# A new order of steps for a fused attention and Fourier-mixing kernel

## The chip, the cores and the metric

The kernel runs on one core of one Trainium2 chip. The metric is the device time of one execution in microseconds. The engines are TensorE (PE, with its weight loads as PEld), VectorE (DVE), ScalarE (ACT), GpSimd (POOL) and SyncE (SP, which here only issues DMAs).

## What is computed

For 4 batches, 8 heads, 768 positions and head size 64, block-sparse attention: each query sees its own block of 64 keys and the three blocks with the highest gate score, causally. Its result, 768 x 512 per batch, goes through a two-dimensional Fourier transform (the real part), a layer norm and a two-layer network with a residual:

```python
gate_scores = np.einsum('bhsd,bhnd->bhsn', q, k_rep)       # k_rep: mean of k over blocks of 64
top_idx = np.argsort(gate_scores, axis=-1)[..., -top_k:]   # causal, top_k = 3, own block always
attn = softmax(scale * q @ k.T under that mask); x = attn @ v
mixed = np.real(np.fft.fft(np.fft.fft(x, axis=1), axis=2)); u = x + mixed
un = (u - mu) / np.sqrt(var + 1e-06)
out = u + np.maximum(un @ w_ch1, 0.0) @ w_ch2              # 512 -> 2048 -> 512
```

## The kernel before

The work is cut into 16 head pairs P (batch P // 4) for the attention and 4 batches b for the rest. Each piece is a named step, and the string `ORDER` lists all steps, `name:arguments`, in one sequence. A loop at the end of the kernel calls each step's function; every engine then executes its own instructions in the order in which the list issues them, whatever the scheduler would choose, and SP its DMAs likewise. So the list is five queues written as one. Engines wait for each other only through the data and through buffers: PSUM has four slots of two banks that tp, g, sc, av, yp, mx, xt, h and c tiles share; the q/k slots `qk_s` are three (P % 3), the v slots four, the loaded q and k have three buffers each, the loaded v two.

The steps, by engine:

- SP: `Lq`, `Lk`, `Lv` load a pair; `un` for batches 1 to 3 is two DMA transposes; `od` stores 128 rows.
- PE: `tk`, `tq` transpose k and q of pair P (L297; up to P = 8 and 6); `g` gate scores (L347, L354); `s:P,i` one of six score tiles (L421 with mask matmuls L433 for P < 7, L426 after that); `v` attention times v (L461); `y:b,h` and `m:b,kp` the two transforms (L531/L537, L564/L565); `xt` transposes of batch 0 (L597); `w:b,it` one of 16 slices of the first layer (L641/L643); `c:b,st,h` half of one row tile of the second layer (L668).
- DVE: `ks`, `kh` block sums of k; `qc` q copied or turned (L328, L326); `kb` turns k; `gt`, `gx`, `gl`, `gm` threshold and mask of the gate (L361/L366, L378, L221, L398); `x` divides the attention (L472, L221); `fs`, `fd`, `f` fold x for the transform (L221 and short copies L506 to L516); `tr` a reversed copy; `u` adds x (L578); `bn`, `nv` statistics (L610 to L621); `un` for batch 0 (L602); `r:b,it` with it % 4 = 3 (L651); `o` scales and adds (L680).
- ACT: `kc` copies k (L317, L320); `e:P,i` the exponential of a score tile (L443); `ty` a copy; `xu` (L590); the other `r` (L653).
- POOL: `qs` q into its slot; `d:P,i` the causal triangle of a tile (L449); `vc` the cast of v; `K` the mask rows for P >= 7 (eight copies through L224); `nr` a Newton iteration (12 small steps); `W`, `X` issue the loads of the weights; `pg:b` copies four elements of the folded tile, so POOL stands there until the fold of batch b is finished (L519).

An attention pair goes through Lk/Lq, tk/tq, ks/kh/qc, g, gt, gx, gl, gm, (K), s, e, d, v, x. A batch goes through fs, fd (pairwise adds and differences), f, y, ty/tr, m, u, xu, un, then w/r, c, o, od, with bn, nv, nr beside w. The pairs of the next batch are interleaved with w and c of the one before.

Of the kernel before, what the change touches and what calls it, by code (L numbers as in the profile page):

```python
# [117 lines left out]
gl:2,1 e:1,2 d:1,3 gm:2 g:3 d:1,4 ks:4 d:1,0 v:0 d:1,5 gt:3 vc:1 kc:4 gx:3 e:1,1 s:2,5 Lv:3 Lq:6
LF:0 Lq:7 Lk:6 Lk:7 LT:0 s:2,3 kh:4 gl:3,0 e:2,5 gl:3,1 s:2,4 e:2,3 d:1,1 x:0 tq:5 qs:4 e:2,4 g:4
d:2,3 gm:3 qc:5 s:2,0 d:2,4 s:2,2 d:1,2 e:2,0 gt:4 d:2,5 tk:5 vc:2 gx:4 e:2,2 s:2,1 ks:5 d:2,0 Lv:4  # L120
Lq:8 Lk:8 s:3,1 e:2,1 v:1 gl:4,0 kh:5 gl:4,1 kc:5 d:2,1 gm:4 d:2,2 s:3,2 x:1 e:3,1 vc:3 g:5 e:3,2
Lv:5 Lc:0 d:3,1 s:3,5 gt:5 s:3,0 fs:0,1 e:3,5 s:3,3 d:3,2 gx:5 e:3,0 s:3,4 fs:1,1 tq:6 gl:5,0 e:3,3
fs:0,0 v:2 gl:5,1 fs:1,0 e:3,4 d:3,3 qc:6 d:3,0 s:4,5 x:2 d:3,4 s:4,4 e:4,5 d:3,5 s:4,0 qs:5 v:3
# [22 lines left out]
un:1,1 un:1,2 un:1,0 od:0,3 Lk:13 Lk:14 od:0,5 Lv:12 od:0,4 Lv:13 Lk:15 Lq:15 od:0,2 w:1,0 x:9 g:12
s:11,2 s:11,4 e:10,5 s:10,4 w:1,12 e:10,3 gt:12 e:10,0 w:1,10 s:11,1 e:10,2 e:11,0 s:11,5 w:1,1
r:1,0 e:11,2 s:10,1 kb:13 ks:13 gx:12 gl:12,0 fs:9,1 gl:12,1 gm:12 kb:14 qc:13 kh:13 fs:9,0 fs:8,0
w:1,8 e:10,4 e:11,4 w:1,11 r:1,12 r:1,11 r:1,10 e:11,5 r:1,1 s:11,3 e:10,1 w:1,6 qc:14 ks:14 kh:14
w:1,15 w:1,13 r:1,8 kc:13 g:14 e:11,3 g:13 e:11,1 r:1,15 gt:13 r:1,6 gx:13 bn:1,4 gl:13,0 gl:13,1  # L150
w:1,5 gm:13 d:11,5 d:10,5 d:10,1 d:10,4 d:10,2 d:11,4 K:12 d:11,3 d:10,3 d:11,2 d:11,0 d:10,0 K:13
# [648 lines left out]
```

## Time and profile before

| | |
|---|---|
| device time, median of 3 runs | 292.67 us (292.5 to 293.05) |
| profiled execution: device time | 292.97 us |
| its span | 291.2 us |
| PE, DVE, ACT, POOL busy | 276.6, 202.9, 163.6, 116.1 us |
| mean granted TensorE clock | 1.0 |

A row of the profile names line, engine, operation, the tile written and the tiles read. "Idle" is the time an engine stood before an instruction, and the releaser is the instruction whose end let it go on. Steps share helper lines (L221 for all two-operand steps, L224 for copies on POOL), so they are told apart by tile. The clock was the same in every stretch.

### The profile page before, as it was taken

To read this page: it belongs to the slowest core of one execution; us is meant where nothing else is said; L and a number is where in the kernel's file an instruction comes from. 1 tells how busy PE (TensorE), PEld (TensorE's weight loads), DVE (VectorE), ACT (ScalarE), POOL (GpSimd) and SP (SyncE) were. 2 spreads that over 40 slices of the span, in tenths; PEclk is the share of its full clock that TensorE was granted. 3 is DMA by queue.
4 is the path that set the end of the run, shared out by engine and by line. 5 is a ranking of instruction groups with operands and counts; after the bars stand their busy time and mean duration, and the time that the engine had idled before them with its cause. 6 is when DMAs were issued, how large, how long until landed. Compare 5 with 4: busy or idle time off the path is not lost.

```text
span 291.2 us, 6585 instructions
## 1 busy us (share of the span) xinstructions
PE 276.6 (95%) x2537; PEld 169.2 (58%) x2537; DVE 202.9 (70%) x604; ACT 163.6 (56%) x205; POOL 116.1 (40%) x286
## 2 busy tenths in 40 slices
PE   8799999899998989999998999999999999999994
PEld 4466777655665465556574466656676454564642
DVE  2999999999996978977899766793566155420231
ACT  3698989865872625978577672864263401353100
POOL 2267527454888650852771798038000000003000
PEclk9999999999999999999999999999999999999999
DMA  9999999998999297259610002543000331000063
GB/s 199 278 225 228 205 200 205 221 170 155 172 174 194 65 222 131 51 123 242 109 41 2 0 7 50 146 91 146 0 2 0 37 109 36 0 2 0 0 237 127
DMA packets 118287, 33.52 MB, mean 115 GB/s; under 512 B 111024, under 2 KB 115056, under 8 KB 118256
## 3 DMA queue, kind: packets, MB, share of 16 engines
q1 hardware_dynamic: 112592, 28.47, 45.0%
q0 software_dynamic: 3664, 4.19, 8.8%
q10 hardware_dynamic: 2000, 0.44, 0.7%
q8 instruction: 20, 0.33, 0.5%
q14 instruction: 11, 0.09, 0.1%
HBM read 28.63 MB, written 6.29 MB: 120 GB/s over the span
## 4 chain that ended last, share of the span: by engine, by line
PE 68%; DVE 17%; ACT 8%; POOL 4%; issue 2%; DVEq 0%; ACTq 0%; POOLq 0%
PE c L668 24%; PE h L641 15%; PE h L643 7%; ACT pt L443 5%; PE sc L426 5%; PE av L461 4%; DVE kr L306 2%; PE yp L531 2%; PE mx L564 2%; POOL pt L449 2%; DVE q L328 2%; PE mx L565 2%; DVE mx L378 1%; PE warmps L705 1%; DVE u L578 1%
## 5 line engine op out<-in xcount | busy, mean ns | idle before, releaser
L443 ACT ACTIVATE pt<-sc 128x1024 f16<-128x1024 f32 (+1 forms) x96 | 82.8, 921 | 28.9 <-PE sc L426 19.8
L641 PE MATMUL h<-unT,w 128*128 128x512 f16 x256 | 84.8, 379 | 2.3 <-DVE hT L651 1.1
L668 PE MATMUL c<-w_sb,hT 128*128 128x512 f16 x368 | 84.0, 379 | 0.5 <-ACT hT L653 0.5
L643 PE MATMUL h<-unT,w 128*128 128x256 f16 x256 | 69.7, 272 | 0.0
L653 ACT ACTIVATE hT<-h 128x768 f16<-128x768 f32 x48 | 37.6, 809 | 51.4 <-PE h L643 51.2
L449 POOL TENSOR_SCALAR_AFFINE_SELECT pt<-pt 128x256 f16<-128x256 f16 x96 | 40.0, 444 | 49.1 <-ACT pt L443 48.6
L668 PEld LDWEIGHTS <-hT 128*128 128x128 f16 x368 | 35.4, 98 | 40.0 <-issue 1.2
L641 PEld LDWEIGHTS <-w 128*128 128x128 f16 x256 | 25.0, 97 | 29.5 <-issue 1.2
L651 DVE TENSOR_SCALAR hT<-h 128x768 f16<-128x768 f32 x16 | 15.1, 948 | 27.3 <-PE h L643 27.3
L680 DVE SCALAR_TENSOR_TENSOR u<-c,rs,u 128x512 f32<-128x512 f32 (+1 forms) x25 | 17.5, 721 | 20.3 <-PE c L668 19.2
L643 PEld LDWEIGHTS <-w 128*128 128x128 f16 x256 | 25.0, 98 | 6.0 <-issue 2.6
L224 POOL TENSOR_SCALAR_AFFINE_SELECT qk<-q 64x768 f16<-64x768 f32 (+1 forms) x25 | 21.5, 862 | 15.0 <-DVE q L328 11.0
L426 PE MATMUL sc<-qk 96*128 96x512 f16 (+3 forms) x144 | 26.2, 306 | 0.0
L224 POOL TENSOR_SCALAR_AFFINE_SELECT qk<-mt 32x160 f16<-32x160 f16 x72 | 23.1, 341 | 7.6 <-DVE mt L398 5.8
L221 POOL TENSOR_TENSOR t<-vr,rs 128x6 f32<-128x6 f32 x12 | 2.9, 242 | 54.5 <-DVE rs L621 53.8
L461 PEld LDWEIGHTS <-pt 128*128 128x128 f16 x672 | 22.4, 97 | 3.0 <-issue 0.8
L461 PE MATMUL av<-v,pt 128*128 128x65 f16 x672 | 23.2, 193 | 0.6 <-POOL v L224 0.6
L578 DVE SCALAR_TENSOR_TENSOR u<-mx,x 128x512 f32<-128x512 f32 x24 | 15.6, 687 | 8.4 <-PE mx L565 8.4
L590 ACT ACTIVATE x<-u,nm 128x512 f16<-128x512 f32 x24 | 15.7, 714 | 9.7 <-DVE nm L584 9.5
L426 PEld LDWEIGHTS <-qk 96*128 96x128 f16 x144 | 13.1, 97 | 9.9 <-issue 1.2
L421 PE MATMUL sc<-qk 64*128 64x512 f16 (+3 forms) x112 | 14.7, 306 | 1.8 <-ACT pt L443 0.8
L610 DVE BATCH_NORM_STATS2 bst<-u 128x6 f32<-128x512 f32 x24 | 16.2, 674 | 0.0
(99 smaller groups left out, 357.2 us busy)
## 6 DMA issues: line engine op xcount, KB each, us to landing
nat<-in_v_dram SPq DMA_DIRECT2D x16, 384.0 KB, 4.3
out_dram<-u SPq DMA_DIRECT2D x23, 256.0 KB, 2.7
nat<-in_q_dram SPq DMA_DIRECT2D x36, 96.0 KB, 4.0
nat<-in_k_dram SPq DMA_DIRECT2D x17, 192.0 KB, 3.4
nat<-in_k_dram SPq DMA_DIRECT2D x28, 96.0 KB, 2.8
nat<-in_q_dram SPq DMA_DIRECT2D x13, 192.0 KB, 3.6
...
```

What stands on the lines that cost most here:

```text
L224: nc.gpsimd.affine_select(out=out, in_=in_, pattern=[[0, i] for i in n], base=0, channel_multiplier=0, compare_op=ALU.is_ge, fill=0.0)
L426: nc.tensor.matmul(ps[:, e, co:co + q1 - q0], qk[0:96, e, 1, 128 * jt:128 * jt + 128], qk[0:96, e, 0, q0:q1], start=True, stop=True)
L443: nc.scalar.activation(out=d["pt"][:, o:o + 2 * n].rearrange("p (e c) -> p e c", e=2), in_=d["sc", i][:, :, 0:n], func=AF.Exp, scale=0.125)
L449: nc.gpsimd.affine_select(out=dg, in_=dg, pattern=[[0, 2], [1, 128]], base=0, channel_multiplier=-1, compare_op=ALU.is_ge, fill=0.0)
L461: nc.tensor.matmul(av[:, e, 66 * st:66 * st + 65], pt[:, co:co + 128], vv[:, e, jt, 0:65], start=(cnt == 0), stop=(cnt == 20))
L578: nc.vector.scalar_tensor_tensor(out=u_b[:, k2, :].rearrange("p (m two) -> p two m", two=2), in0=mps[:, k2, :].rearrange("p (two m) -> p t ...
L610: nc.vector.bn_stats(out=bst, in_=u_t[b, kt // 2][:, kt % 2, :])
L641: nc.tensor.matmul(hp[:, 0:512], w1s, unT[:, dt, 0:512], start=(dt == 0), stop=(dt == NDT - 1))
L643: nc.tensor.matmul(hp[:, 512:768], w1s, unT[:, dt, 512:768], start=(dt == 0), stop=(dt == NDT - 1))
L653: nc.scalar.activation(out=hT, in_=hp, func=AF.Relu)
L668: nc.tensor.matmul(c_ps[b, g[0]][:, st - g[0], :], h_t[b, it][:, 128 * st:128 * (st + 1)], w2_sb[:, it, :], start=(it == 0), stop=(it == N ...
L680: nc.vector.scalar_tensor_tensor(out=o, in0=ps, scalar=st_t[b][1][:, st:st + 1], in1=o, op0=ALU.mult, op1=ALU.add)
```

## The change

The set of steps and everything each step does stay the same, as do the constants and first loads ahead of the list. Only `ORDER` differs, from its first line to its last: every engine's queue, and SP's, has another order, made with the knowledge that VectorE and GpSimd can lock each other out. The core of the diff (old lines first, then new ones; each "..." stands for lines left out):

```diff
@@ ORDER = """
-Lk:1 Lq:1 Lk:2 Lq:2 tk:0 ks:0 tq:0 Lq:3 Lk:3 kh:0 qc:0 iz:1 tk:1 qs:0 kc:0 g:0 ks:1 iz:0 gt:0 tq:1
-kc:1 gx:0 Lq:4 Lv:0 Lk:4 Lv:1 kh:1 gl:0,0 tk:2 gl:0,1 gm:0 kc:2 qc:1 s:0,3 s:0,2 ks:2 e:0,3 qs:1
...
-fs:3,0 s:5,2 fd:2,1 e:5,0 fd:3,1 s:4,3 fd:3,0 e:5,2 tk:6 f:0,1 f:0,2 e:4,3 Lk:9 Lq:9 tk:7 f:0,3
-e:4,2 f:0,0 y:0,1 ks:7 pg:0 W:0 kc:6 y:0,0 tr:0,1 d:4,0 kc:7 d:4,4 d:4,5 ks:6 d:5,5 d:4,1 ty:0,1
-tr:0,0 s:5,3 d:5,2 s:5,4 d:4,3 kh:6 W:1 ty:0,0 m:0,2 qs:6 e:5,3 u:0,2 m:0,1 vc:4 e:5,4 m:0,0 u:0,1
-xu:0,2 d:5,4 tk:8 d:5,1 d:4,2 u:0,0 xu:0,1 d:5,0 xt:0,2 W:2 g:6 un:0,2 xu:0,0 xt:0,1 gt:6 un:0,1
-kc:8 xt:0,0 qc:8 un:0,0 qs:8 v:4 Lq:10 Lk:10 Lv:6 Lq:11 qc:7 bn:0,3 gx:6 w:0,1 gl:6,0 r:0,1 w:0,2
-gl:6,1 gm:6 r:0,2 w:0,5 s:6,0 s:6,3 w:0,6 ks:8 kh:7 x:4 kh:8 bn:0,4 g:8 g:7 fs:4,1 s:6,1 r:0,5 e:6,0
...
-bn:0,0 bn:0,2 ks:10 gl:9,0 fs:5,1 nv:0 gl:9,1 e:7,1 s:7,2 e:7,2 gm:9 qs:9 K:8 d:7,3 d:6,3 d:6,2
-d:6,5 d:6,0 d:7,4 vc:6 d:7,2 d:6,1 d:7,5 X:1 qs:10 K:9 vc:7 d:7,0 d:7,1 nr:0 kc:9 s:8,3 w:0,9 r:0,9
-w:0,14 r:0,14 w:0,11 v:6 s:8,5 r:0,11 kh:10 w:0,15 g:10 e:8,3 e:8,5 c:0,0,0 x:6 s:9,1 v:7 s:8,4
-fs:6,1 gt:10 c:0,1,0 s:8,2 c:0,2,0 s:8,1 s:8,0 r:0,15 fs:6,0 x:7 c:0,0,1 s:9,5 c:0,1,1 fs:7,0 gx:10
-fs:7,1 fd:7,1 fs:4,0 fd:6,0 qc:11 fd:7,0 fd:6,1 f:1,1 f:1,0 f:1,2 f:1,3 y:1,1 e:9,1 e:8,4 e:8,2
...
-vc:8 vc:9 d:8,3 d:8,1 d:8,4 d:9,5 qs:11 d:8,5 d:9,1 d:9,3 d:9,4 d:8,0 d:9,0 vc:10 K:10 qs:12 d:9,2
-pg:1 K:11 vc:11 v:8 s:10,5 c:0,4,1 s:10,3 s:10,0 x:8 o:0,4 o:0,5 kb:12 ks:12 kh:12 v:9 s:10,2 s:11,0
...
-c:1,0,1 s:12,3 e:12,5 e:13,4 s:13,0 e:12,3 s:13,1 kc:15 e:13,1 c:1,1,1 c:1,4,0 e:13,0 gx:15 fs:8,1
-fs:11,1 fd:11,1 gl:15,0 fd:10,0 fd:11,0 fd:10,1 f:2,1 f:2,2 gl:15,1 gm:15 f:2,0 f:2,3 nr:1 d:12,0
-d:12,1 d:13,3 d:13,2 d:13,5 d:12,3 qs:15 d:12,5 d:12,4 d:12,2 vc:12 d:13,0 K:15 K:14 pg:2 d:13,1
-d:13,4 vc:13 y:2,0 v:12 c:1,4,1 ty:2,0 y:2,1 o:1,0 s:15,3 tr:2,0 c:1,5,0 ty:2,1 m:2,0 c:1,5,1 o:1,1
...
+Lk:1 Lq:1 Lk:2 Lq:2 Lq:3 Lk:3 tk:0 kc:0 ks:0 tq:0 iz:0 kh:0 qc:0 tk:1 ks:1 g:0 iz:1 kc:1 tq:1 tk:2
+gt:0 gx:0 gl:0,0 gl:0,1 kh:1 gm:0 kc:2 qc:1 qs:0 qs:1 Lq:4 Lv:0 Lk:4 Lv:1 Lq:5 Lk:5 s:0,3 tq:2 s:0,4
...
+e:5,3 f:0,3 f:0,2 gx:6 f:0,0 gl:6,0 f:0,1 y:0,1 qc:8 gl:6,1 tr:0,1 y:0,0 e:5,2 tr:0,0 e:4,1 e:5,1
+tk:8 ks:8 gm:6 e:4,4 m:0,2 kh:7 W:0 W:1 d:4,2 pg:0 d:4,1 d:4,3 vc:4 d:4,0 d:4,4 d:4,5 d:5,3 W:2 v:4
+u:0,2 ty:0,1 ty:0,0 m:0,0 s:6,2 x:4 u:0,0 kc:8 g:7 kh:8 m:0,1 gt:7 xu:0,2 xt:0,2 e:6,2 u:0,1 s:6,5
+s:6,0 xu:0,0 e:6,5 un:0,2 s:6,1 xt:0,0 gx:7 s:6,3 un:0,0 e:6,0 g:8 gl:7,0 xu:0,1 gt:8 xt:0,1 s:6,4
+s:5,0 un:0,1 w:0,9 e:6,3 e:5,0 bn:0,3 gl:7,1 gm:7 kb:9 bn:0,1 e:6,4 w:0,2 Lq:10 Lk:10 Lv:6 Lq:11
+d:6,0 vc:5 d:5,1 qs:8 d:5,4 d:5,2 K:7 d:5,0 d:5,5 X:0 d:6,5 qs:7 Li:0 Lv:7 Lq:12 Lv:8 Lv:9 r:0,2
...
+ks:10 kh:10 r:0,10 g:9 w:0,1 r:0,11 qc:11 r:0,14 w:0,13 gt:9 gx:9 gl:9,0 bn:0,2 nv:0 gl:9,1 gm:9
+d:7,5 d:7,2 d:6,2 d:6,3 d:7,0 d:6,4 qs:9 X:1 vc:6 d:7,3 K:8 d:6,1 d:7,1 vc:7 d:7,4 K:9 nr:0 r:0,13
+w:0,0 r:0,0 v:6 r:0,1 s:8,4 e:8,4 s:8,3 x:6 w:0,7 v:7 e:8,3 s:8,5 qc:10 fs:6,1 r:0,7 c:0,0,0 s:9,4
+s:8,1 e:8,1 c:0,1,0 c:0,1,1 s:9,0 e:9,4 e:9,0 c:0,0,1 s:9,1 x:7 fs:7,1 fs:6,0 fd:6,1 fs:5,1 fd:6,0
+fs:7,0 fd:7,1 fd:7,0 f:1,3 f:1,2 Lv:10 Lv:11 Lk:11 Lq:13 Lq:14 Lk:12 g:10 e:8,5 y:1,1 s:8,2 f:1,1
...
+ks:12 kh:12 u:1,0 kc:12 xu:1,0 gl:11,0 g:12 c:0,4,1 gt:12 u:1,2 gl:11,1 gm:11 xu:1,2 d:8,3 vc:8
+d:8,4 vc:9 pg:1 vc:10 qs:11 d:8,5 d:8,0 d:9,4 d:9,3 K:10 vc:11 qs:12 qs:10 d:8,1 d:9,2 d:8,2 d:9,5
+K:11 d:9,0 d:9,1 od:0,2 od:0,1 od:0,0 Lk:13 un:1,1 un:1,0 un:1,2 Lk:14 Lv:12 Lv:13 Lk:15 Lq:15
...
+fd:10,1 gm:14 s:13,4 c:1,1,0 s:12,1 c:1,1,1 e:13,4 gl:15,0 f:2,3 gl:15,1 f:2,0 f:2,2 gm:15 bn:1,2
+nv:1 f:2,1 e:13,3 c:1,0,1 y:2,1 e:13,1 e:12,1 y:2,0 tr:2,0 kc:15 ty:2,1 kc:14 c:1,4,0 ty:2,0 c:1,5,0
+s:13,2 e:13,2 d:12,0 d:12,2 d:12,4 K:14 d:12,3 d:13,5 d:12,1 nr:1 d:13,3 qs:15 d:12,5 K:15 d:13,4
+d:13,0 d:13,2 qs:14 pg:2 d:13,1 v:12 s:15,4 o:1,1 c:1,5,1 s:15,1 tr:2,1 m:2,1 e:15,4 o:1,0 x:12
...
```

More of the change, by code (lines that the diff above doesn't have):

```diff
@@ L118 @@
[L118 to L123, printed above, removed]
@@ L146 @@
[L146 to L151, printed above, removed]
@@ new lines @@
+kb:13 e:10,5 v:9 s:11,0 e:10,1 e:11,0 w:1,0 r:1,0 s:11,2 w:1,10 s:11,1 x:9 e:11,2 s:11,5 e:11,5
+w:1,2 s:10,0 w:1,15 s:10,4 e:11,1 w:1,13 fs:9,0 gl:12,1 s:11,4 o:0,5 s:11,3 kb:14 ks:13 r:1,15
+bn:1,4 ks:14 r:1,2 kh:13 fs:9,1 bn:1,1 qc:14 gm:12 w:1,1 w:1,12 e:10,0 e:10,4 g:13 gt:13 r:1,10
+w:1,11 e:11,4 gx:13 gl:13,0 r:1,11 gl:13,1 gm:13 e:11,3 bn:1,5 d:11,5 vc:13 d:10,1 qs:13 d:10,4
+vc:12 d:11,2 d:10,5 d:10,3 d:10,2 d:11,1 d:10,0 d:11,3 d:11,4 K:12 d:11,0 K:13 v:10 x:10 kh:14 w:1,5
+w:1,14 r:1,13 w:1,7 kc:13 s:12,5 w:1,4 r:1,12 s:12,2 r:1,1 r:1,5 v:11 e:12,5 r:1,14 s:13,5 s:13,0
@@ new lines @@
+c:2,4,1 o:2,0 u:3,0 u:3,1 u:3,2 c:2,3,1 xu:3,1 xu:3,0 xu:3,2 od:1,3 od:1,2 od:2,0 od:2,1 un:3,0
+un:3,2 un:3,1 w:3,11 w:3,3 w:3,4 r:3,4 o:2,4 w:3,14 o:2,5 bn:3,2 bn:3,3 w:3,2 w:3,8 bn:3,0 r:3,11
+bn:3,5 w:3,9 r:3,14 r:3,2 o:2,2 w:3,5 r:3,9 w:3,10 r:3,3 r:3,8 bn:3,1 w:3,12 bn:3,4 r:3,12 w:3,1
+w:3,15 nv:3 pg:3 nr:3 w:3,6 r:3,1 w:3,0 w:3,7 o:2,3 r:3,6 r:3,0 r:3,5 r:3,15 r:3,7 c:3,0,0 c:3,2,0
+w:3,13 r:3,10 r:3,13 c:3,5,1 c:3,2,1 c:3,4,0 c:3,4,1 o:3,2 o:3,6 c:3,1,0 o:3,4 c:3,1,1 o:3,1 c:3,3,0
+c:3,3,1 o:3,3 c:3,0,1 o:3,0 c:3,5,0 o:3,5 od:3,6 od:3,2 od:2,2 od:2,3 od:2,4 od:2,5 od:3,1 od:3,4
@@ L177 @@
+od:3,3 od:3,0 od:3,5
 """
```

64 lines of the change are left out of this document (31 added, 33 removed).

## The prediction

> **What bounds the kernel now.** I read the page first, then the busy time by stretch, TensorE's (PE's) waits, and the chain. The page:
>
> ```profile
> PE 276.6 (95%) x2537; PEld 169.2 (58%) x2537; DVE 202.9 (70%) x604; ACT 163.6 (56%) x205; POOL 116.1 (40%) x286
> ```
>
> PE has 95%, so an order can only win what PE waits. Where that is shows in the busy time of four stretches (columns: stretch, its length, then PE, PEld, DVE, ACT, POOL, each with its count, the clock and the DMA):
>
> ```profile
> 5.80:57.80 52.00, 46.89 (x727) 34.38 (x726) 49.32 (x164) 45.70 (x57) 26.23 (x52) 1.00 1.08 225
> 57.80:103.20 45.40, 43.45 (x413) 25.55 (x413) 40.59 (x137) 27.39 (x34) 32.32 (x73) 1.00 0.91 158
> 103.20:173.50 70.30, 67.77 (x579) 40.20 (x580) 58.20 (x181) 49.35 (x61) 37.57 (x87) 1.00 0.46 91
> 173.50:287.20 113.70, 113.69 (x809) 66.92 (x809) 53.63 (x118) 39.64 (x52) 18.34 (x60) 1.00 0.22 60
> ```
>
> Up to 57.8 us, where the first w (w:0,1) starts, DVE is the bound: 49.32 of 52.00 busy, only 2.7 idle. From 57.8 to 173.5 PE is nearly full: it waits 1.95 + 2.53 = 4.5 us. From 173.5 on it doesn't wait at all, so everything that is gained or lost before 173.5 goes straight to the end.
>
> PE's idle time is a little more than these 4.5 us, because the end of a matmul is drawn late:
>
> ```profile
> L668 PE MATMUL c<-w_sb,hT 128*128 128x512 f16 x368 | 84.0, 379 | 0.5 <-ACT hT L653 0.5
> ```
>
> and in the chain, one c step, eight of them back to back:
>
> ```profile
> 94.26 1.73 PE c L668 x8
> ```
>
> 1.73 / 8 = 0.216 us from one to the next, 0.379 drawn: each gap is 0.16 us longer than its row. With some 15 gaps after 57.8 that makes 4.5 + 2.4 = **6.9 us lost after 57.8**. Whom PE waited for (total, times, longest):
>
> ```profile
> PE h L641 <- DVE hT L651: 1.1, 1, 1.1
> ```
>
> ```profile
> PE av L461 <- POOL v L224: 0.6, 1, 0.6
> PE yp L531 <- DVE fg L513: 0.5, 1, 0.5
> PE sc L421 <- DVE kr L306: 0.5, 2, 0.3
> PE yp L531 <- DVE fg L516: 0.5, 1, 0.5
> ```
>
> Each of these five ends in a DVE or POOL step, and ahead of each the lock shows. Before the first (PE waits at 88.4), DVE and then POOL in order of time:
>
> ```profile
> 84.35 1.02 DVE L221 TENSOR_TENSOR sd<-x 128x384 f16<-128x384 f16 x1
> 85.29 0.79 DVE L617 TENSOR_SCALAR vr<-mv 128x6 f32<-128x6 f32 x1
> 86.11 0.17 DVE L619 TENSOR_SCALAR rs<-vr 128x6 int32<-128x6 int32 x1
> 86.32 0.68 DVE L621 TENSOR_SCALAR rs<-rs 128x6 int32<-128x6 int32 x1
> ```
>
> ```profile
> 84.24 0.89 POOL L739 DMA_DIRECT2D w_sb<-in_moe_w_ch_dram  x1
> 85.14 1.83 POOL L224 TENSOR_SCALAR_AFFINE_SELECT qk<-q 64x768 f16<-64x768 f32 x2
> ```
>
> Three steps on six elements: one takes 0.17, its neighbours 0.79 and 0.68 beside POOL's qs, and the 384-wide fold takes 1.02 beside X:0. About 1.7 us too much, and hT (r:0,11) stands behind them on DVE. The same ahead of y:1,1 and y:1,0:
>
> ```profile
> 102.69 0.38 DVE L513 COPY fg<-zw 128x6 f16<-128x6 f16 x1
> 102.97 0.55 DVE L221 TENSOR_TENSOR fg<-zw 128x762 f16<-128x762 f16 x1
> 103.44 0.80 DVE L516 COPY fg<-zw 128x6 f16<-128x6 f16 x1
> ```
>
> ```profile
> 100.13 2.90 POOL L449 TENSOR_SCALAR_AFFINE_SELECT pt<-pt 128x256 f16<-128x256 f16 x4
> 102.99 2.10 POOL L224 TENSOR_SCALAR_AFFINE_SELECT qk<-q 64x768 f16<-64x768 f32 x2
> ```
>
> POOL's d steps take 0.72 here; their group, and the chain ahead of v:12 (PE's POOL wait at 173.5), say what they cost elsewhere:
>
> ```profile
> L449 POOL TENSOR_SCALAR_AFFINE_SELECT pt<-pt 128x256 f16<-128x256 f16 x96 | 40.0, 444 | 49.1 <-ACT pt L443 48.6
> ```
>
> ```profile
> 165.75 2.40 POOL pt L449 x4
> ```
>
> **What the lock is worth.** Behind it stand the waits 1.1, 0.6, 0.5, 0.5, and the larger half of the kr ones (0.3), with 0.16 each: 3.0 + 0.8 = 3.8 of the 6.9 us. That is the most that knowing the lock can bring, short of other improvements; the other 3.1 us are waits for ACT and for DVE in ordinary queues.
>
> **What the change moves after 57.8.** No instruction is added or removed; only places in the five queues move. (1) pg:1, POOL's tiny copy that waits for batch 1's fold f, stood behind all of d:8 and d:9; now only d:8,3, vc:8, d:8,4 and vc:9 stand ahead of it. The rest (qs:11, K:10, ten d) can't run beside f:1 any more. Who waits for them: s:10,2 needs qs:10 and K:10. Ahead of these, POOL then has three qs (3 x 1.83), two vc (the nearest row is the 0.92 of half a qs: 1.8), four d (4 x 0.44) and K:10, a memset and eight copies of
>
> ```profile
> L224 POOL TENSOR_SCALAR_AFFINE_SELECT qk<-mt 32x160 f16<-32x160 f16 x72 | 23.1, 341 | 7.6 <-DVE mt L398 5.8
> ```
>
> (2.7 us and a little): 12 us. PE has y:1,0, six c (6 x 1.73 = 10.4 us), three m, g:11, g:12 and three s between f:1's end and s:10,2, over 15 us, so the cover holds; if it went, PE would stand for the difference. The y:1 waits go. (2) r:0,11 now stands ahead of nv:0 on DVE, and x:6 behind it, so a slow nv:0 no longer stands between hT and a w. (3) nr:1 stands behind most of d:12 and K:14 and behind the end of most of f:2; v:12 still needs d:12,5, behind nr:1 and qs:15. vc:12, for which PE waited, stands a whole group of POOL work earlier. I take all 3.8 us as gone, and of the other 3.1 us 2.2 as staying: w and s steps are spread differently and I can't show that these waits vanish; followed by hand, POOL arrives within half a microsecond of PE at s:7,5 and v:6. SP's loads, od's and transposes move too (three od ahead of un:1); no row of PE's waits names a DMA, and v:8, v:9 and three c lie between m:1,2 and w:1,0, which covers the transposes, with landing at
>
> ```profile
> unT<-x SPq DMA_TRANSPOSE x18, 2.5
> ```
>
> after issue; if that cover went, it would cost about one landing.
>
> [...]
>
> **What the change moves before 57.8.** This is against it. In the old order DVE finishes un:0,0, the last step that w:0 needs, and only then takes qc:7 and so on:
>
> ```profile
> 57.09 0.65 DVE unT L602
> 57.74 0.88 DVE q L326
> ```
>
> The new order puts these DVE steps ahead of the last un of batch 0 (un:0,1): qc:7, gx:6, gl:6,0, gl:6,1, ks:8, gm:6, kh:7, x:4, kh:8, gt:7, gx:7, gl:7,0, gt:8. Their prices, from the chain and, for x, the groups:
>
> ```profile
> 59.41 0.62 DVE mx L378 x9
> ```
>
> ```profile
> 61.25 0.48 DVE mt L398
> 61.73 0.85 DVE kr L306
> ```
>
> ```profile
> 144.32 0.36 DVE gt L366
> ```
>
> ```profile
> 144.86 0.79 DVE mx L378 x10
> ```
>
> ```profile
> 146.66 0.23 DVE ltb L221
> ```
>
> ```profile
> L221 DVE TENSOR_TENSOR x<-av,rcp 128x768 f16<-128x768 f32 x16 | 15.3, 958 | 0.6
> ```
>
> qc 0.88, gx 0.62 + 0.79, ks 0.85, gm 0.48, two gt 2 x 0.48 (the 0.36 and three short memsets before the next step at 144.86), x 0.96 and its reciprocal like a small one, with these six small ones of 0.23: 6.9 us. W:0 and W:1, which POOL issues, now stand ahead of pg:0 and so may run beside f:0; X:0 above stretched a fold to 1.02, against 0.55 for the wider step of f:1, so some 0.5 us each, which I leave to the bounds. And at the start, where ACT's copy of the transposed k (kc:0) and DVE's sum over it (ks:0) follow one another:
>
> ```profile
> 7.60 0.80 ACT L317 CAST qk<-tp 128x768 f16<-128x768 f32 x1 [0.45 <-DVE kr L306]
> ```
>
> The copy waited for the sum; now kc:0 stands first, so ks:0 and all of DVE behind it start 0.8 us later. Together 7.7 us. DVE's own 2.7 us of idle time in this stretch could absorb part: bounds +7.7 (nothing) and +5.0 (all). I take +6.2, nearly the middle, as no row excludes either end: w:0,9 starts at 64.0. On the other side PE does more ahead of it: s:6,0 to s:6,5, g:7, g:8:
>
> ```profile
> 64.62 0.68 PE g L354 x16
> 65.30 0.32 PE sc L421 x4
> ```
>
> ```profile
> 66.23 0.32 PE h L641
> ```
>
> two g in 0.68, two s in 66.23 - 65.30 = 0.93, so five large s, one small and two g make 3.1 us. Net loss before w:0: 6.2 - 3.1 = **+3.1 us** (bounds +1.9 and +4.6).
>
> **Sum.** +3.1 - 3.8 - 0.9 = -1.6 us on a span of 291.2: 289.6. The profiled execution took 292.97, 1.8 beyond its span, and lies 0.3 above the median 292.67: 292.67 - 1.6 = **291.1**.
>
> **Rivals.** (a) Slower: DVE's longer queue ahead of batch 0 is not won back. The price is the +3.1, and the 6.9 us of later waits stay in sum, since the other waits grow into the room that the lock's leave: 292.67 + 3.1 = 295.8. For it: DVE was full for 95% of that stretch, and the 6.9 us of steps are certain. Against: after w:0 DVE has 6.9 us less to do. It decides from the point where more than 3.8 us of the later waits remain. (b) POOL takes the lock's place: its queue is now just in time at s:7,5, v:6 and s:15,4; one half qs (0.92) late at each is 2.8 us more than forecast: 293.9. For it: POOL is gated behind pg:1 and was busy for 32.32 of 45.40 already; against: it had 40% over the span. (c) Better: nothing waits after w:0: 292.67 + 3.1 - 6.9 = 288.9, and 287.7 if DVE's idle time absorbs all it can. [...]
>
> **How the numbers follow.** Forecast 0.48, (a) 0.22, (b) 0.11, (c) 0.14, (d) 0.05. 0.2% is 0.6 us, about what a measurement of this kernel can tell from no change. The forecast's own range is 288.2 (the early term at +1.9 and 1.7 us more of the later waits gone) to 292.6 (the early term at +4.6): 0.37 of its share lies below 292.1, 0.09 within 0.2%, 0.02 above. The range of 8 in 10 goes from 287.7, the end of (c), to 295.8, the price of (a), past which lies a good half of (a)'s share. Faster: 0.37 + 0.14 = 0.51; within 0.2%: 0.09; slower: 0.02 + 0.22 + 0.11 + 0.05 = 0.40.
>
> **What would show it.** In the trace after: the first w at 63 to 65 with DVE above 95% until there; the short fold steps of f:1 at 0.17 and no wait of yp for fg near y:1; no POOL wait at v:12; PE without a gap from v:12 on, where 114 us follow. Wrong would be: the first w before 62 (the early term is mis-sized), waits of PE for K, qs or d of over 2 us in sum (rival b), or PE's later gaps still near 7 us (rival a).

## The result and the profile after

| | before | after |
|---|---|---|
| median of 20 runs | 292.69 us | 294.48 us |
| all runs | 291.19 to 302.85 | 292.02 to 297.30 |
| profiled execution | 292.97, span 291.2 | 293.81, span 292.1 |

The ratio is 1.005, with an interval of 1.003 to 1.0069: slower by 1.8 us between the medians (1.5 by the ratio), where 291.1 was forecast. About half of it stands in the profile (0.9 us of span, at full clock); the rest lies in runs in which TensorE's clock fell: twelve of the 20 runs have a mean granted clock of 0.997 or more and spans of 290.3 to 293.4 us (mean 291.9), the other eight a clock of 0.992 to 0.994 and spans of 293.9 to 295.6 (mean 294.7). All ratios leave out executions over 1.5% above the fastest of their kernel, and so do, below, the times of h1_old_start (295.86 us with its one of 571) and k1_ks_first (295.21 with its one of 721).

The first line of after's page, and its busy time in the stretches that answer to those of before (the first now ends at 64.8, shortly before the new first w, w:0,9):

```profile
PE 275.1 (94%) x2537; PEld 169.5 (58%) x2537; DVE 197.3 (68%) x604; ACT 165.3 (57%) x205; POOL 114.2 (39%) x286
```

```profile
5.80:64.80 59.00, 49.06 (x785) 36.26 (x785) 54.11 (x200) 48.61 (x60) 26.26 (x50) 1.00 1.07 213
64.80:103.20 38.40, 37.63 (x337) 22.76 (x333) 32.27 (x86) 23.63 (x29) 28.68 (x68) 1.00 1.01 163
103.20:173.50 70.30, 69.14 (x604) 41.70 (x602) 55.83 (x196) 49.70 (x61) 38.79 (x95) 1.00 0.47 86
173.50:288.00 114.50, 114.50 (x808) 66.65 (x805) 53.94 (x119) 41.89 (x54) 18.79 (x57) 1.00 0.21 63
```

DVE's sum fell by 5.6 us (202.9 to 197.3) for the same instructions: they were stretched less. Behind 64.8 PE waits 0.8 + 1.2 us, where it waited 4.5. But ahead of the first w PE stands idle for 9.9 us instead of 5.1. Whom it waited for, the largest rows:

```profile
PE tp L297 <- ACT pt L443: 2.5, 2, 1.7
PE tp L297 <- DMA nat<-in_k_dram: 1.5, 3, 0.6
PE g L347 <- DVE q L328: 1.2, 1, 1.2
PE h L641 <- ACT pt L443: 1.1, 2, 0.7
PE sc L421 <- ACT pt L443: 1.0, 3, 0.5
PE sc L433 <- DVE mt L398: 0.9, 1, 0.9
PE sc L421 <- DVE x L221: 0.8, 1, 0.8
PE tp L297 <- DMA nat<-in_q_dram: 0.5, 1, 0.5
PE mx L564 <- ACT pt L443: 0.4, 1, 0.4
```

The waits behind the lock (by which I mean steps of VectorE and GpSimd that take longer beside each other: 0.79 and 0.80 us for VectorE steps of 0.17, 0.72 for GpSimd's d of 0.41, in before's rows) are gone. The loads (`nat`, 2.0 us) are new, the waits for ACT's exponential (`pt`) have grown from 1.4 to 5.9 us over the whole list, and the waits ahead of the first w that a DVE step ended from 2.4 to 2.9.

To compare kernels I use one account throughout, counted from tk:0 on. For every PE step I take the usual time from its start to the start of the next (the lower quartile over the steps of its kind); what a step starts later than the sum of those ahead of it is **lost**. Of the profiles:

| kernel | first w at | lost by then | lost at the end |
|---|---|---|---|
| before | 57.8 | 8.7 | 16.2 |
| after | 65.2 | 13.0 | 16.9 |
| p1_old_pg | 57.8 | 8.7 | 14.6 |
| p2_lock | 57.3 | 8.7 | 13.5 |
| bank_p2 | 56.7 | 7.6 | 10.8 |
| h3_seam | 57.8 | 8.7 | 13.5 |
| rows_before | 59.1 | 10.0 | 17.0 |
| rows_after | 65.7 | 13.6 | 15.3 |
| sums_after | 65.1 | 12.9 | 16.9 |
| bank_after | 67.4 | 14.6 | 17.5 |

So the change loses 4.3 us up to the first w (13.0 - 8.7) and wins 3.6 behind it (16.2 - 8.7 = 7.5 against 16.9 - 13.0 = 3.9).

### The profile page after: what moved, and what is told of

Same layout as the page of the kernel before. It is cut to its first block, busy times and chain, and to the rows that moved or that the text cites. A ratio compares the mean times of both kernels' runs of the same rounds, so it can differ in the third digit from the quotient of the medians.

```text
span 292.1 us, 6586 instructions
## 1 busy us (share of the span) xinstructions
PE 275.1 (94%) x2537; PEld 169.5 (58%) x2537; DVE 197.3 (68%) x604; ACT 165.3 (57%) x205; POOL 114.2 (39%) x286
## 4 chain that ended last, share of the span: by engine, by line
PE 70%; DMA 9%; SPq 6%; POOL 5%; DVE 3%; ACT 3%; issue 3%; ACTq 0%; POOLq 0%; DVEq 0%
PE c L668 26%; PE h L641 15%; PE h L643 8%; PE sc L426 6%; PE av L461 5%; DMA nat<-in_k_dram 5%; DMA nat<-in_q_dram 4%; SPq L282 3%; POOL qk L224 3%; SPq L277 2%; ACT pt L443 2%; POOL pt L449 2%; PE mx L564 1%; PE yp L531 1%; PE mx L565 1%
## 5 line engine op out<-in xcount | busy, mean ns | idle before, releaser
L449 POOL TENSOR_SCALAR_AFFINE_SELECT pt<-pt 128x256 f16<-128x256 f16 x96 | 38.8, 427 | 59.2 <-ACT pt L443 56.5
L426 PE MATMUL sc<-qk 96*128 96x512 f16 (+3 forms) x144 | 27.7, 305 | 0.1
L224 POOL TENSOR_SCALAR_AFFINE_SELECT qk<-q 64x768 f16<-64x768 f32 (+1 forms) x25 | 20.8, 834 | 17.6 <-DVE q L328 12.2
L224 POOL TENSOR_SCALAR_AFFINE_SELECT qk<-mt 32x160 f16<-32x160 f16 x72 | 24.0, 355 | 6.7 <-DVE mt L398 5.1
L297 PE MATMUL tp<-id,nat 128*128 128x128 f32 x96 | 13.2, 279 | 4.5 <-ACT pt L443 2.5
L224 POOL TENSOR_SCALAR_AFFINE_SELECT v<-nat 128x768 f16<-128x768 f32 x16 | 15.2, 949 | 4.7 <-DMA nat<-in_v_dram 4.5
```

Of the source, the lines that this page charges most:

```text
L224: nc.gpsimd.affine_select(out=out, in_=in_, pattern=[[0, i] for i in n], base=0, channel_multiplier=0, compare_op=ALU.is_ge, fill=0.0)
L426: nc.tensor.matmul(ps[:, e, co:co + q1 - q0], qk[0:96, e, 1, 128 * jt:128 * jt + 128], qk[0:96, e, 0, q0:q1], start=True, stop=True)
L449: nc.gpsimd.affine_select(out=dg, in_=dg, pattern=[[0, 2], [1, 128]], base=0, channel_multiplier=-1, compare_op=ALU.is_ge, fill=0.0)
```

## The experiments

All kernels but the five whose names begin with rows_, bank_ and sums_ differ from before or after in `ORDER` alone. Line numbers in their rows are those of the kernel itself: one less in h2_new_start, eight or nine more in the bank_ and sums_ kernels.

### Crossing the two orders

**h1_old_start** and **h2_new_start**: one order up to the first w, then the steps that are left in the order of the other.

```diff
 h1: <before, up to gx:6>  + <all other steps as after has them>
 h2: <after, up to un:0,1> + <all other steps as before has them>
```

> The list is the old one up to the first w, and from there all steps that are left in the new order. Theory A (two terms that can be parted: the new start costs PE 4.3 us up to the first w, the new order behind it saves 3.4): PE loses 8.7 us up to the first w, as in the old kernel, and about 4 after it, so 292.7 - 3.4 = 289.3 us. Rival B (the later waits only shrank because the other engines stood further ahead of PE after the slow start): the later waits come back to about 7 us, 292.5 us. First w at 58 us in both.

> The reverse: the new list up to the first w, then the steps that are left in the old order. Theory A: first w at 65 us, later waits of PE 7 us as in the old kernel: 292.7 + 4.3 = 297.0 us. Rival B: later waits near 4 us by themselves, since PE comes later: 293.6 us.

h1: 295.57 us, ratio 1.009 (1.0058 to 1.0121). h2: 303.1, ratio 1.0289 (1.0241 to 1.0336). Neither theory fits. A second profile of h1:

> The same kernel as h1_old_start, taken again for a profile: old list up to w:0,1, the remaining steps in the new order; its time was 295.86 us against 292.87 before. Theory A (what a list loses is set by the seam): the start up to 57.8 us repeats the old one, 8.7 us lost at the first w, and the other 5 to 6 us that separate it from 289.3 stand as PE gaps within 30 us behind the seam, one of them long enough to lower the granted clock (0.987 is about two stretches of 3.4 us at half speed, 2 x 1.7 us). Theory B (the new order's later part is no better than the old one): the gaps are spread from 57.8 to 173.5 us, 9 us in sum, none over 1.3 us, and the clock is full in every stretch.

295.06 us, clock 0.987. PE's matmul in order of time at 61.86 us, and the busy time from 58 to 66 (the figure behind POOL's is the granted clock):

```profile
61.86 0.56 PE L433 MATMUL sc<-mt,indz 64*128 64x224 f16 x4 [3.96 <-DVE mt L398]
```

```profile
58.00:60.00 2.00, 0.00 (x0) 0.00 (x0) 1.97 (x12) 0.00 (x0) 1.34 (x3) 1.00 1.29 223
60.00:62.00 2.00, 0.14 (x2) 0.13 (x3) 1.93 (x7) 0.00 (x0) 0.00 (x0) 0.51 1.22 199
62.00:64.00 2.00, 2.00 (x26) 0.89 (x24) 1.79 (x11) 1.30 (x2) 0.00 (x0) 0.50 0.68 116
```

It is the seam. The new order puts s:6,2 ahead of the w's, since its DVE has done gm:6 by then; behind the old start DVE hasn't, PE stands still for 3.96 us, and the clock is at half from 60.0 to 66.9, of which PE still waits 1.9. Leave the seam out (4.3 us lost there, and about 2 by the clock), and h1 loses 3.3 us from w:0,9 on, like after's 3.9. Its seam cost hides what its start is worth. h2 has a bad seam too: its first w comes at 69.1, and between 60 and 100 us PE waits 5.8 us, 2.7 of them for ACT's hT. Ahead of that, PE at tk:8 of h2:

```profile
55.10 0.85 PE L296 MATMUL tp<-id,nat 128*128 128x128 f32 x6 [2.84 <-DMA nat<-in_k_dram]
```

```profile
56.00:58.00 2.00, 2.00 (x26) 1.74 (x24) 2.00 (x6) 1.01 (x2) 0.00 (x0) 0.57 1.11 191
58.00:60.00 2.00, 2.00 (x33) 1.86 (x31) 1.19 (x6) 1.72 (x3) 0.00 (x0) 0.58 1.14 234
```

A load that lands late, a gap of 2.84 us, then 3.4 us at half clock: that is 1.7 us of work, and 1.7 of 292 makes a mean clock of 0.994, as this profile has it; eight of after's 20 runs show 0.992 to 0.994. What the clock follows is not shown. The length of the gap alone doesn't decide it: in pg_late's profile 3.4 us at half clock begin at the end of a gap of 1.58 us, while t2_late's profile below has a gap of 3.10 us at full clock.

### The lock alone, in the old order

**p1_old_pg**, then **p2_lock** on top of it:

```diff
 p1: -... d:8,2 vc:8 vc:9 d:8,3 ... d:9,2 pg:1 ...
     +... d:8,2 vc:8 vc:9 pg:1 d:8,3 ... d:9,2 ...
 p2: +... vc:12 nr:1 d:12,0 ...            (vc:12 was behind d:12,2)
     +... s:8,5 r:0,11 nv:0 nr:0 kh:10 ... (nv:0 and nr:0 were ahead of it)
```

> The old order with POOL's gate pg:1 moved ahead of ten of its d steps, as in the new order. Theory A (the lock is what PE waited for at y:1): the short fold steps of f:1 take 0.17 instead of 0.38 and 0.80, PE's two waits there (1.3 us together) go, 292.7 - 1.3 = 291.4 us. Rival D (POOL's work that is held back by the gate is late for s:10 and v:8 instead): these waits come back there, 292.7 us or more.

> p1_old_pg (the old order with pg:1 ahead of d:8,3) with two more steps placed by the lock: vc:12 ahead of nr:1 on POOL, which is idle there for 7 us, and nv:0 and nr:0 behind r:0,11, so that its short steps beside POOL's qs no longer stand ahead of hT. Theory A (each wait behind the lock can be taken alone): the waits of 1.1 us at w:0,15 and 0.6 us at v:12 go, with 0.16 us each, 2.0 us in sum: 289.5. Theory B (the waits only move to the next step, as nearly all engines are full at 88 us): half of it at most, 290.5 to 291.5.

p1: 291.5 us (291.17 to 291.84), ratio 0.9944 (0.9925 to 0.9964). p2: 289.79, ratio 0.9894 (0.9869 to 0.9919). Theory A, both times. Of p1's waits, these two are what p2 then takes away, and p2's list has neither:

```profile
PE h L641 <- DVE hT L651: 1.1, 1, 1.1
PE av L461 <- POOL v L224: 0.6, 1, 0.6
```

Three moves by the lock are worth 2.9 us, nearly what the prediction took for these waits (3.3, all but kr), and they don't touch the start.

**pg_late** undoes the first of them in the new order:

```diff
-vc:9 pg:1 vc:10 ... d:9,0 d:9,1 od:0,2
+vc:9 vc:10 ... d:9,0 d:9,1 pg:1 od:0,2
```

> The new order with one part undone: pg:1, POOL's copy that waits for batch 1's fold, behind all of d:8 and d:9 (behind d:9,1) instead of ahead of ten of them. Theory A (the waits of y:1 go because POOL holds still beside the fold; worth 1.4 us in the old order, p1_old_pg): the waits of yp for fg come back, and the time rises by 0.7 to 1.5 us, 295.2 to 296.0. Theory B (in the new order the other moves have already taken these waits): 294.2 to 294.8, and no wait of yp for fg.

294.9 us, ratio 1.0066 (1.0037 to 1.0095), no wait of yp for fg: Theory B by the waits, 0.1 us above its range by the time. PE's only wait in its profile from 95 to 115 us is one of 0.4 us for ACT's exponential. So in the new order the gate that the prediction named is not what takes these waits away.

### VectorE's queue ahead of the first w

**k1_ks_first** undoes the swap at the start, **t1_late** and **t2_late** take DVE steps behind the first w, **ks6_first** fills an idle stretch of DVE:

```diff
 k1:  -tk:0 kc:0 ks:0 tq:0 iz:0 kh:0 qc:0      +tk:0 ks:0 tq:0 iz:0 kh:0 qc:0 kc:0
 t1:  +w:0,9 kh:7 ks:8 kh:8 x:4 g:7 gt:7 gx:7 gl:7,0 g:8 gt:8 e:6,3   (all from ahead of un:0,1)
 t2:  +w:0,9 qc:7 kh:7 kh:8 g:7 gt:7 gx:7 gl:7,0 g:8 gt:8 e:6,3       (likewise)
 ks6: -ks:7 ks:6 ... kc:7 ... kc:6             +ks:6 ks:7 ... kc:6 kc:7
```

> The new order with one step moved: the copy of k of pair 0 (kc:0) behind the sum over it (ks:0) and the copy of q, as in the old order. Theory A (VectorE's queue bounds the first stage, and it starts 0.8 us later): the first w comes 0.8 us earlier than 65.2, and the time falls by 0.8 us against the new order's. Rival C (the loads bound the first stage: PE waits there for the DMAs of k): first w stays at 65 us within 0.3, time as the new order's.

> The new order with eight VectorE steps of pairs 7 and 8 and the two g that feed them (kh:7, ks:8, kh:8, x:4, g:7, gt:7, gx:7, gl:7,0, g:8, gt:8) moved behind w:0,9: 4.3 us of VectorE's queue ahead of batch 0's last un are gone, and 0.7 us of PE's cover. Theory A (VectorE's queue sets the first w): the first w starts 3.0 to 4.3 us earlier than 65.2, 61 to 62, and the time falls by 2.3 to 3.6 us less what comes back later: 291 to 293. Theory B (loads, PSUM banks and the copies of ScalarE set it, and VectorE only looks full because it is filled): the first w starts at 64 or later and the time stays at 294 to 295.

> The new order again with work of pairs 7 and 8 moved behind w:0,9, but only steps that keep no PSUM bank occupied while they wait: qc:7, kh:7, kh:8, g:7, gt:7, gx:7, gl:7,0, g:8 and gt:8 (3.3 us of VectorE's queue, 1.4 us of PE's); ks:8 and x:4, which free a bank, stay where the new order has them. Theory A (t1_late lost its 11 us because two of the four banks stayed occupied, and VectorE's queue does set the first w): the first w at about 62, 291.5 to 293. Theory B (VectorE's queue does not set the first w): the first w at 64 or later, 294 to 297.

> The new order with two swaps: on VectorE ks:6 ahead of ks:7, on ScalarE kc:6 ahead of kc:7. In the new order VectorE stands 1.5 us idle at 38.4 for tk:7, while ks:6, whose input is there since 37.3, is queued behind. Theory A (VectorE is the bound before the first w, and what it idles there is lost): 0.9 us less at the first w, 293.3 to 293.8, and fewer runs with a clock under 0.997. Theory B (the first w hangs on PE's chain through tk:7 and the banks): no change, 294.2 to 294.8.

k1: 295.0 us, ratio 1.0069 (1.0045 to 1.0092): no gain from that swap. Its profile is that of the 721 us, so its first w isn't known. t1: 305.6 (1.0394 to 1.0458); t2: 298.06 (1.0138 to 1.019); ks6: 295.42 (1.0046 to 1.0114). None gained. t1 shows why a step can't be moved for its engine's sake alone: ks:8 and x:4 each free one of the four PSUM places, and PE then waited for places:

```profile
PE xt L597 <- ACT pt L443: 1.8, 2, 1.1
PE sc L421 <- DVE unT L602: 1.6, 2, 0.8
```

In t2 and ks6, PE waits 3.10 and 2.40 us at tk:8 for its load, which hides what the moves did. So **sums_after** leaves every queue as it is and makes DVE's steps shorter:

```diff
+        w = 16 if P < 8 else 64
         nc.vector.tensor_reduce(out=kr12, in_=ps.rearrange("p (n c) -> p n c", c=64)
+                                [:, :, 0:w],
```

> The new order, with the same PSUM places as it has (written out), and VectorE's sums over the transposed k (ks) of pairs 0 to 7 taken over 16 of each 64 elements, so that a step of 0.9 us takes about 0.3; the block sums are thus not the reference's. Some 5 us of VectorE's work ahead of the first w are gone, and every queue keeps its order. Theory Q (VectorE's queue sets the first w): 61 to 62 instead of 65.2, and the time falls by 3 us or more, to 291.5 or less. Theory C (the chain of loads, PE, ScalarE and the four places sets it): the first w at 64 or later, 293.5 or more.

296.35 us, ratio 1.012 (1.0087 to 1.0153), and its busy time up to 64.8:

```profile
5.80:64.80 59.00, 49.55 (x786) 36.63 (x786) 50.69 (x200) 48.42 (x60) 26.05 (x50) 1.00 1.06 215
```

DVE does 3.4 us less, and the first w starts at 65.1 instead of 65.2: Theory C. y:0,1 does come 0.9 us earlier, at 49.2, and DVE is ready for tk:8 by as much; but tk:8 stands at 53.4 as in after, since its load lands then, and DVE now stands 1.33 us for it instead of 0.47:

```profile
54.25 0.96 DVE L315 TENSOR_REDUCE kr<-tp 128x12 f32<-128x768 f32 x1 [1.33 <-PE tp L305]
```

So this run too meets the late load, and it shortens only steps ahead of tk:8. It shows that DVE's queue up to there doesn't hold the first w by itself; it can't show what DVE's queue would do without the load.

### The loads

PE's idle time of the start is lost ahead of tk:8: 8.9 us in after (4.0 in before), and 1.0 from tk:8 to the first w in both. In after and sums_after tk:8 starts when its k has landed. The two loads of pair 8's k, from issue to landing, in before, after and sums_after:

```profile
L282 SPq DMA_DIRECT2D nat<-in_k_dram x2: 475/509/543, 42.8 to 43.3; - x2
DMA to landing us min/median/max: 2.7/2.8/2.9
```

```profile
L282 SPq DMA_DIRECT2D nat<-in_k_dram x2: 528/679/830, 43.1 to 43.7; - x2
DMA to landing us min/median/max: 9.5/9.6/9.6
```

```profile
L290 SPq DMA_DIRECT2D nat<-in_k_dram x2: 528/635/742, 42.8 to 43.4; - x2
DMA to landing us min/median/max: 9.6/9.7/9.8
```

Issued at the same time, they take 9.6 us instead of 2.8. What else is under way differs: the loads of the first layer's weights, which POOL issues. Before, then after:

```profile
45.53 0.96 POOL L735 DMA_DIRECT2D w<-in_moe_w_ch_dram  x1
49.02 0.77 POOL L735 DMA_DIRECT2D w<-in_moe_w_ch_dram  x1
```

```profile
41.75 1.72 POOL L735 DMA_DIRECT2D w<-in_moe_w_ch_dram  x2
50.93 0.18 POOL L519 COPY gone<-fg 1x4 f16<-1x4 f16 x1 [3.10 <-DVE fg L221]
```

In the old list W:0 and W:1 stand behind pg:0, so POOL issues them at 45.5 and 49.0; in the new one ahead of it, so both start at 41.8, 1.3 us ahead of pair 8's k. They are 512 and 768 KB; at the 174 and 193 GB/s that the DMA engines moved from 40 to 50 and from 50 to 60 us that is 7 us, about what the k loads take longer (6.8). The other profiles agree: the slower of these two loads took 9.6 to 12.4 us in the eight kernels with the new start that issue it there, and 2.9 to 5.2 in the six with the old start. No kernel moves W:0 and W:1 alone, so that they are the reason is a reading.

**l8_early** issues pair 8's loads ahead of v's:

```diff
-Lv:4 Lq:8 Lk:8 gt:4
+Lk:8 Lq:8 Lv:4 gt:4
```

> The new order with one change on SP's queue: the loads of k and q of pair 8 (Lk:8, Lq:8) issued ahead of the v load of pair 4 (Lv:4), k first; all steps of the computing engines stay as they are. tk:8 is the one transpose of the new order whose load lands last (PE waits for it at 53.4 us, 0.6 us in the profile). Theory A (the clock): in 8 of the new order's 20 runs the mean clock was 0.992 to 0.994, since that wait grows to near 3 us there and the clock then falls to half for one stretch; with the load some 8 us earlier the wait goes in every run, all clocks are 0.998 or more, and the median falls from 294.5 to 292.5 to 293.2 us. Theory B (the low clock comes from gaps that no load makes, those for PSUM banks and for VectorE): clocks of 0.993 stay in a third of the runs and the median stays at 294.0 to 294.8.

294.64 us, ratio 1.0047 (1.0021 to 1.0072), five of twelve runs with a low clock: Theory B by the time. k's loads, now issued ahead of W:0, land within 5.2 us, and PE no longer waits at tk:8; the loads of v, now issued beside W:0 and W:1 (from 42.7 us on), take 12.0 and 12.9 us, and POOL waits for one at vc:4:

```profile
POOL v L224 <- DMA nat<-in_v_dram: 2.1, 1, 2.1
```

Yet tk:8 starts at 53.5 as in after, and the first w no earlier than there:

```profile
65.75 0.39 PE L641 MATMUL h<-unT,w 128*128 128x512 f16 x1
```

For this the trace has a plain reason. From the end of tk:7 to the last un, DVE (the third busy figure) works without a gap, 23.69 of 24.16 us:

```profile
40.72:64.88 24.16, 20.52 (x366) 16.01 (x363) 23.69 (x80) 21.86 (x29) 9.54 (x19) 1.00 1.05 183
```

The chain that ends in the first w runs over DVE's steps all that way. So with the load out of the way DVE's queue sets the first w, and with a shorter queue (sums_after) the load does. The two limits lie close together (in after DVE stood only 0.47 us for tk:8), and no kernel takes both away. A third is near: in t2_late DVE does 2.1 us less behind tk:8, but the first w comes 11.4 us behind tk:8 instead of 11.7, since the chain then goes over ACT's xu and e.

**rows_after** and **rows_before** change the form of the loads of q and k, so that each partition gets its 3 KB in one piece:

```diff
-            eng.dma_start(t[:, :, e, :], src[b, 2 * hp + e].rearrange("(st p) d -> p st d", p=128))
+            eng.dma_start(t[64 * e:64 * e + 64].rearrange("p st e d -> p (st e d)"),
+                          src[b, 2 * hp + e].rearrange("(p n) d -> p (n d)", p=64))
```

> The new order with the loads of q and k (pairs 1 to 15) changed in their form alone: each partition gets one piece of 3 KB of consecutive rows, instead of 256 or 128 bytes at a time; number and bytes of the loads are the same, the rows come in another arrangement, so what is computed is not the reference's. All queues keep their order. Theory L (the new order's start hangs on the loads: it wants them earlier than the old one, all 16 DMA engines are busy until 60 us, and how late they land differs from run to run): PE's waits for loads ahead of the first w go, the first w comes at 61 to 63 instead of 65.2, all clocks are 0.997 or more, the runs lie within 1 us of one another, and the time is 290 to 292, at or below rows_before plus 0.5. Theory Q (VectorE's queue and the PSUM banks set the start, the loads are beside it): the first w stays at 64 to 65, low clocks stay, 293.5 to 294.5, 1.5 us or more above rows_before.

> The old order with the same change of the loads' form (rows in another arrangement, the same bytes), as the base for rows_after. Both theories: PE waits for hardly any load in the old order ahead of the first w, so it gains little: 291.5 to 292.7, the first w at 57 to 57.8.

rows_after: 292.17 us, ratio 0.997 (0.9949 to 0.9991); rows_before: 293.56, ratio 1.0019 (1.0001 to 1.0037). The new order is now the faster one by 1.4 us, as Theory L has it, but not by its reason: the first w comes at 65.7, PE waits longer for loads (6.0 us against 2.0), and seven of twelve runs still have a low clock. What was gained lies behind 90 us. PE at w:0,7, in after and in rows_after, behind the same steps:

```profile
92.04 0.38 PE L641 MATMUL h<-unT,w 128*128 128x512 f16 x1 [0.71 <-ACT pt L443]
```

```profile
91.66 0.38 PE L641 MATMUL h<-unT,w 128*128 128x512 f16 x1
```

The queues of PE, DVE, ACT and POOL are the same in both. What differs is which of the four PSUM places each result gets: that is settled when the program is built, and for 136 of 246 results it came out differently. So this pair doesn't test the loads alone.

### The places

**bank_after** and **bank_p2** write the places out by hand, each result into the one that came free first in the profile of the same order:

```diff
+    banks = iter(BANKS)      # a string of 246 digits
     def pst(shape, name, dtype=FP):
-        return psump.tile(shape, dtype, tag="ps", name=name)
+        return psump.tile(shape, dtype, tag=f"ps{next(banks)}", name=name, bufs=1)
```

> The new order with nothing changed but which of the four PSUM tiles of two banks each result is put into: the list of 246 places is written out by hand, each result into the place that came free first by the profile of the new order, instead of the place that was settled when the program was built. Theory P (places): at w:0,7 PE waits until 92.0 for a place while another is free since 87.0, and so at m:1,1 and w:1,1; these three waits (1.9 us with the 0.16 each) and the one at s:5,4 (0.9) go, the later loss falls from 3.9 to about 2.0 us, and the time is 291.7 to 292.7. Theory L (rows_after was faster because its loads are cheaper): 294.2 to 294.8, with the same waits.

> p2_lock (the old order with three lock fixes) with the places written out in the same way, by its own profile. Its waits at w:1,15, w:1,7, w:1,14 and c:1,0,0 (2.0 us in sum) are for a place while another has been free for 0.3 to 3.3 us. Theory P: all four go, 287.6 to 288.2. Theory W (behind each of them the next thing is late as well, hT or un): 288.8 to 289.8.

bank_p2: **288.55 us** (287.61 to 288.94), ratio 0.9842 (0.9814 to 0.9871), the fastest of all. The profiled execution (287.69) lies in the range of Theory P; the median lies between those of P and W. All four waits are gone from its profile, and one of 0.5 us for POOL is new. Its busy time from the first w to 172 us:

```profile
57.30:100.00 42.70, 42.25 (x408) 24.99 (x407) 38.27 (x135) 27.38 (x34) 28.73 (x67) 1.00 1.00 162
100.00:172.00 72.00, 71.38 (x641) 43.26 (x640) 59.42 (x187) 49.74 (x61) 41.58 (x101) 1.00 0.51 99
```

PE waits 1.1 us in 115. bank_after gained nothing: 294.66 us, ratio 1.0067 (1.0039 to 1.0094). Its waits at w:0,7, m:1,1 and w:1,1 are gone, as Theory P has it; but v:10 waits 1.3 us for POOL, ten of twelve runs have a low clock, and ahead of the first w its profile shows this. DVE, and POOL beside it:

```profile
51.18 2.43 DVE L229 TENSOR_TENSOR lt<-lt,oth 128x108 f16<-128x108 f16 x1
```

```profile
50.50 0.76 POOL L457 TENSOR_SCALAR_AFFINE_SELECT pt<-pt 128x256 f16<-128x256 f16 x2
51.21 0.89 POOL L232 TENSOR_SCALAR_AFFINE_SELECT v<-nat 128x768 f16<-128x768 f32 x1
52.07 1.47 POOL L457 TENSOR_SCALAR_AFFINE_SELECT pt<-pt 128x256 f16<-128x256 f16 x4
```

and the same step in after:

```profile
51.75 0.17 DVE L221 TENSOR_TENSOR lt<-lt,oth 128x108 f16<-128x108 f16 x1
```

A step of 0.17 us took 2.43. In its profile POOL's vc:4 is drawn 0.03 us behind the start of DVE's step, in after's 0.04 and in those of six more kernels with the new start (h2_new_start, t1_late, t2_late, ks6_first, pg_late, rows_after) 0.04; in those seven the step took 0.17. So the rows don't show what decided. Here the step ended at 53.61, 0.07 us behind the last of POOL's vc and four d in a row (0.89 and 1.47 us, drawn to 53.54).

**calm_after** takes away that race and, as l8_early does, the late load:

```diff
-Lv:4 Lq:8 Lk:8 gt:4      -gl:6,0 f:0,1 y:0,1 qc:8 gl:6,1 tr:0,1
+Lk:8 Lq:8 Lv:4 gt:4      +gl:6,0 gl:6,1 f:0,1 y:0,1 qc:8 tr:0,1
```

> The new order with the two places made safe where its profiles differ from one another ahead of the first w: the loads of pair 8 go ahead of Lv:4 (as in l8_early), and VectorE's gl:6,1 stands ahead of the last fold step f:0,1 instead of behind qc:8. In bank_after's profile that step of 108 elements took 2.43 us instead of 0.17, since POOL, let go by pg:0, had begun vc:4 and four d 0.03 us after the step was due; in the new order's own profile it was ahead by 0.04 us. Theory R (a race between the two engines, and a late load, make the spread and the low clocks): no run with a clock under 0.997 but for one or two in twelve, spans within 1.5 us, and the median falls from 294.5 to 292.5 to 293.3. Theory S (spread and low clocks come from the stall at tk:6 and tk:7, 34 to 40 us): low clocks stay in a third of the runs, 294.0 to 294.8.

294.77 us (1.0041 to 1.0089), seven of twelve clocks under 0.997: Theory R falls. gl:6,1 takes 0.22 us here, but vc:4 waits 3.3 us for its load, and PE 5.7 us for loads in all. Which loads are late differs from kernel to kernel; that some are is common to them.

### A seam that fits

**h3_seam**: p2_lock up to 91 us, then the new order.

```diff
 <p2_lock, up to fs:6,1> gt:10 + <all other steps as after has them>
```

> The old list with its three lock fixes (p2_lock) up to fs:6,1 at 91 us and gt:10, where the two lists have done nearly the same work (7 us of steps differ instead of 16 to 20 at the first w), and from there the remaining steps in the new order. Theory A (the losses of the parts add where the seam fits: 9.9 us up to w:0,15 in p2_lock, 2.7 from there on in the new order): 12.6 us lost against 13.5 in p2_lock, 288.9, clock full. Theory B (the new order's gain after the first w hangs on its own start, so any seam costs): 290 to 293, with a wait of over 0.5 us within 15 us behind the seam.

290.34 us, ratio 0.9912 (0.9894 to 0.9929): Theory B, with a wait of 1.05 us at s:9,4, two steps behind the seam. The new order's later part, put behind the old start, is as good as p2_lock's (13.5 us lost in both), not better.

## Why the prediction was wrong

The sum was +3.1 - 3.8 - 0.9 = -1.6 us. By the account it came out as +4.3 - 3.6 = +0.7, and low clocks add 1.1 in the mean. These three misses (1.2, 1.1 and 1.1 us) make the 3.4 us between 291.1 and 294.5; the first two alone turn the sign.

- **Where time can be won: right.** PE is without a gap from 173.5 on (114.50 of 114.50), no later wait gave anything back.
- **What the lock is worth: right for the old order.** 3.8 us at most, 3.3 of it without kr; p2_lock took 2.9 us out of the old order by three moves. In after, PE doesn't wait for hT, for batch 1's fold or at v:12. That pg:1 is what does it at the fold was wrong for the new order (pg_late).
- **The start, +3.1 us: too small, 4.3 measured.** The step that failed let DVE's idle time absorb part of its longer queue: 6.9 us of moved steps and 0.8 at the start, less 1.5 of the 2.7 us of idle time, were to put the first w 6.2 us later. It came 7.4 us later (65.2 instead of 57.8). Ahead of it DVE did 4.8 us more, and its idle time didn't shrink but grew by 2.2, to 4.9 us: 92% busy and not above 95%. Of the idle time 1.52 us are at tk:7 and 0.47 at tk:8. Ahead of tk:6 and tk:7, PE waits 1.74 and 0.74 us for a PSUM place that ACT's exponentials free:

```profile
36.47 0.85 PE L297 MATMUL tp<-id,nat 128*128 128x128 f32 x6 [1.74 <-ACT pt L443]
38.98 0.85 PE L297 MATMUL tp<-id,nat 128*128 128x128 f32 x6 [0.74 <-ACT pt L443]
```

```profile
39.87 1.82 DVE L306 TENSOR_REDUCE kr<-tp 128x12 f32<-128x768 f32 x2 [1.52 <-PE tp L297]
```

That DVE's queue carries the first w was neither wrong nor the whole of it: l8_early shows it doing so, sums_after shows the load of tk:8 in its place. What first makes tk:6 late stays open. In after and l8_early the place comes last, in sums_after and calm_after at nearly the same time the load of its k (1.29 and 1.74 us).
- **Loads were left out.** The sentence "no row of PE's waits names a DMA" was true of before, and I let it carry for after, where they end 2.0 us of PE's waits, 0.6 of them at tk:8. Of W:0 and W:1, moved ahead of pg:0, I counted the lock and not the 1.28 MB that they put on the same 16 DMA engines just ahead of pair 8. The landing times show what is issued beside and behind them landing late (9.6 us in after, 12.0 and 12.9 in l8_early); but pair 8's is one of four late loads in after's start, and the loads for tk:6 and tk:7 were issued before W:0.
- **Later waits, 4.7 us less: too much, 3.6 measured.** The step that failed took the other 3.1 us for waits "for ACT and for DVE in ordinary queues", of which 2.2 stay. Three of them (0.5, 0.4 and 0.3, with 0.16 each 1.7 us) were waits for one of four PSUM places while another stood free: they stand in p2_lock's list as in before's, and go in bank_p2 with the places alone. In after, the same kind stands at other steps (w:0,7, m:1,1 and w:1,1, 1.9 us, gone in bank_after). They don't follow from the order alone, so no walk along the queues could tell which stay.
- **The clock: not in the prediction at all.** It was 1.0 in every stretch of before. In the new order it falls in 8 of 20 runs, which are 2.8 us longer than the others, 1.1 us in the mean of all. What makes one run differ from the next is not settled: neither the load of tk:8 (l8_early) nor the step gl:6,1 beside POOL (calm_after) alone.
- **Rivals.** (a), slower because the start is not won back, had the sign and, with 3.9 us of later waits left, just the point from which it decides (3.8); its price of 295.8 was too high, as part of them did go. (b) did not happen: no wait for K, qs or d in after's list is over 0.3 us. Nor did (d), 2.7 us for the four POOL steps ahead of pg:1 beside batch 1's folds: they did run beside the folds (two d of 0.52 and 0.51 us, two vc of 1.22), and one fold took 1.04 us instead of 0.35, but f:1's short steps took 0.17 and PE waited for no fold.
